# A key of their own for attention's values, values and next scores in one TensorE step, and a third buffer for x2's sums

## The chip, the cores and the metric

The kernel runs on one core of a Trainium2 chip, in one launch. The metric is the time of one execution on the device in microseconds (us). The same execution that was profiled gave the trace; all rows below come from it. TensorE is called PE in the rows, VectorE DVE, ScalarE ACT, GpSimd POOL and SyncE SP (it only issues DMAs here).

## The reference

Three layers follow each other on 8 sequences of 576 positions and 512 features, 4,608 positions in all.

```python
# attention, in chunks of 64 positions, 8 heads of 64
scores = scale * matmul(q_c, k_c.T)
scores = scores - max(scores)
attn = exp(scores);  attn = attn / (sum(attn) + 1e-9)
x = matmul(attn, v_c)
# first feed-forward
xn = (x - mu) / sqrt(var + 1e-6) * g_ln
x2 = x + maximum(xn @ w_ch1, 0) @ w_ch2
# gated layer
h = gelu(x2 @ w_in);  u, v = halves of h
v_n = (v - mu) / sqrt(var + 1e-6) * g_ln
v_s = w_sg @ v_n (over the 576 positions) + b_sg
out = x2 + (u * v_s) @ w_out
```

## The kernel before

**Tiles and stages.** The 4,608 positions are 36 tiles t of 128 rows; two tiles make one of 18 blocks b. Phase 1 does attention and the first feed-forward and writes x2 to a scratch tensor in HBM (`x2d`). Phase 2 does the gated layer in four groups of nine tiles and reads x2 back. Large products are computed in fp16 as a high and a low half, three matmuls for one; from block 4 on, and in phase 2, seven products of sub-blocks stand for eight, for which sums of sub-blocks are made first.

**Attention of a tile** (`attention`, lines 265 to 351). SP loads q and k into `qk` or `qkl` (L328) and v into `v` or `vl` (L329). TensorE makes the scores (L296, 16 matmuls of 64x64 in fp32; the rows count each as two), DVE takes their maximum (`mx`, L331) and subtracts it (`pm`, L332), ACT does the exponential (L335), TensorE transposes (L306), DVE sums (`sm`, L337, and L324, L325), ACT copies the transposed tile out (`pt`, L339), TensorE makes the values (L315, again 16 matmuls of 64x64), and DVE multiplies them into `x` (L345). `norm` follows: statistics (L376, L377), normalised `xn` (L379), its halves, and a transposing DMA into `xT`. From tile 6 on all tiles use one pair of PSUM banks, `pair1`: the scores lie in one half of each bank, the values in the other, but both halves have one key. So the scores of tile t+1 wait until `x` of tile t has been read.

**First feed-forward.** Blocks 0 to 3 run `ff1` (L537) and `ff2` (L558), with x2 put together at L570. From block 4 on `ff1p` (L647) writes bank 2 or 3, ACT takes it out (L662), DVE makes the sums (L669 to L671), ACT and POOL or DVE make the halves (L674, L676), and `ff2p` (L698) multiplies by the second weight. Each output tile is stored to `x2d` by SP (L576), and its largest value is taken (L203). Between block 3 and 4 `sums_w2` prepares the second weight (L592 and L602 on DVE, L607 and L608 on ACT, L611 and L612 on POOL). `prep` prepares the weights of phase 2; `par` (L229 to L241) turns a column of maxima into one number in all partitions, with two small TensorE steps, `turn` (L208) and `spread` (L220), and two DVE steps, `rowmax` (L212) and `floor` (L225). Late uses of `par` share `pair1`.

**Phase 2.** `x2_piece` loads two x2 tiles into a buffer `xs` (L919), DVE makes three sums (L926 to L928), ACT and DVE make the halves (L943, L953), and transposing DMAs follow (L941). A unit of v makes seven products (L1250), taken out by ACT (L1156) and DVE (L1160); then come v's ninth tile (L1275), u (L1292, L1313), the mixing over positions (L1346, L1347) and the output product (L1425), which DVE adds to `xr`, x2 loaded a second time (L1428, L1433).

**What sets the order.** Both phases are written as operations with an engine, an assumed duration, the keys they read and write, a priority and a distance `lat`, the assumed time until another engine may use the result. `Plan.run` plays this through: on each engine, of the operations that are ready at that time the one with the smallest priority goes next. The order thus made is fixed in the program; a step that comes late on the chip holds all that stand behind it on its engine. `plan` orders phase 1 and `plan2` phase 2.

Of the kernel before, what the change touches and what calls it, by code (L numbers as in the profile page):

```python
# [132 lines left out]
def fused_kernel(ctx: ExitStack, tc, qkv, w1, w2, g1, w_in, w_out, wsgt, wsgs, g2, b_sg, out):  # L133
# [95 lines left out]
    def par(dst, src, rd, wr, pr):  # L229

        nscr[0] += 1
        if pr < 1000:
            k, c = f"scr{nscr[0] % 3}", nscr[0] % 3 * 160
            scr = bank[6][:, c:c + 160]
        else:
            k, scr = "pair1", pair[1][:, 0, 0:160]
        pr = min(pr, 500)
        op("PE", 130, lambda: turn(scr, src), rd=rd + ["ident"], wr=[k], prio=pr, lat=300)
        op("DVE", 260, lambda: rowmax(scr), rd=[k], wr=["rowm"], prio=pr)
        op("PE", 130, lambda: spread(scr), rd=["rowm"], wr=[k], prio=pr, lat=300)  # L240
        op("DVE", 130, lambda: floor(dst, scr), rd=[k], wr=wr, prio=pr)  # L241
# [21 lines left out]
    xT_t = {}  # L263

    def attention(t):
        early = t < 8
        n = t % 2 if t < 6 else 1
        s2, ks = pair[n], f"pair{n}"
        pr = TUNE['a'][t] if t < 8 else 10 * t
        lat = TUNE['g'][2] if t < 8 else 300 if t < 12 else 1300  # L270
        z = 1

        def o(eng, ns, fn, **k):
            ns = COST.get((eng, ns), ns)
# [28 lines left out]

# [31 lines left out]
        o("ACT", 520, lambda: nc.scalar.activation(out=pm.t, in_=pm.t, func=AF.Exp, scale=0.125), wr=[pm])  # L335
# [7 lines left out]
        ), rd=[ks], wr=[pt])  # L343
        o("PE", 1260 * z, pv_, rd=[pt, v], wr=[ks])
# [5 lines left out]
        ), rd=[ks, rd], wr=[x])  # L350
# [432 lines left out]
    def prep(nm, srcs):  # L783
# [19 lines left out]
        op("DVE", 70, lambda: absmax(redc[:, i:i + 1], mxc[:, i, 0:n]), rd=[f"mxc{i}"], wr=[f"redc{i}"], prio=pr)  # L803

        def sums(k, uv):
            a, c = (full(k + 2 * y)[:, uv * 512:uv * 512 + 512].rearrange("p (h e) -> p h e", h=2) for y in range(2))
            t = winT(k, uv).rearrange("p a n e -> p (a n e)").bitcast(F32).rearrange("p (n e) -> p n e", n=4)
            for o, x, y in (
                (t[:, 0], a[:, 1], a[:, 0]), (t[:, 1], c[:, 1], t[:, 0]),
                (t[:, 2], c[:, 1], a[:, 1]), (t[:, 3], c[:, 0], t[:, 1]),  # L810
            ):
                nc.vector.tensor_tensor(out=o, in0=x, in1=y, op=ALU.subtract)

        if nm == "win":
            for k in range(2):
                for uv in range(2):
                    op("DVE", 1400, lambda k=k, uv=uv: sums(k, uv), rd=[ck[k], ck[k + 2]], wr=[f"winT{k}{uv}"], prio=pr)
# [83 lines left out]
    def x2_make(pl, g, p, pr):  # L901
# [67 lines left out]
    with tc.manual_schedule():  # L969
# [128 lines left out]
        gl = fixed("gl", 1, [P, 4, GT * P], F16)  # L1098
        fixed("hx", 4, [P, 7 * 256], F16)
# [451 lines left out]
```

## Time and profile before

| | |
|---|---|
| median of 3 runs | 1243.23 us (1242.81 to 1244.31) |
| the profiled execution | 1242.74 us |
| its span in the trace | 1241.0 us |
| TensorE busy | 1202.6 us, 97% |
| VectorE, ScalarE, GpSimd busy | 67%, 45%, 35% |
| TensorE clock, mean granted share | 0.992 |

TensorE's matmuls are pipelined, so a "busy" TensorE may still be slower than it could be; its idle time is what the gaps in its row show. The granted clock is 1.00 at 2.4 GHz and 0.50 at 1.2 GHz. A row of the waits names the instruction that waited and the one whose end released it.

### The profile page before, as it was taken

How to read it: one execution, taken by the hardware profiler on the slowest of the kernel's cores; microseconds unless marked ns; L12 is line 12 of the kernel's file. 1: busy time of each engine (PE TensorE's matmuls, PEld its weight loads, DVE VectorE, ACT ScalarE, POOL GpSimd, SP SyncE). 2: the span in 40 equal slices, each digit the busy share in tenths (PEclk: the TensorE clock that was granted, in tenths of full speed). 3: DMA queues.
4: the chain of work that ended last, by engine and by line, in shares of the span. 5: the costliest groups of instructions: out<-in, count | busy, mean ns of one | idle time of the engine just before them, and what ended most of it. 6: DMA issues, size and time to landing. Idle time of an engine off the chain costs nothing. (4 is left out here: it accounts for less than half of the span.)

```text
span 1241.0 us, 27021 instructions
## 1 busy us (share of the span) xinstructions
PE 1202.6 (97%) x11412; PEld 890.7 (72%) x11412; DVE 828.5 (67%) x1545; ACT 561.7 (45%) x844; POOL 439.4 (35%) x425
## 2 busy tenths in 40 slices
PE   7899999899999999999999999998999999999998
PEld 5688654678888888888888888887565357457453
DVE  7786124988967678646555665676688669558445
ACT  6676402455664474343433334344645435435321
POOL 3461401654555474434543344333302302302200
PEclk9999999999999999999999999999999899999999
DMA  9863002244321312322232120345146392382202
GB/s 325 243 200 111 1 34 67 71 167 137 119 69 53 78 43 87 83 56 64 58 69 61 52 61 18 81 109 152 38 104 160 108 170 79 110 137 69 85 1 85
DMA packets 140665, 118.33 MB, mean 95 GB/s; under 512 B 104960, under 2 KB 113152, under 8 KB 140544
## 3 DMA queue, kind: packets, MB, share of 16 engines
q1 hardware_dynamic: 140544, 116.61, 34.9%
q8 instruction: 89, 1.46, 0.5%
q14 instruction: 32, 0.26, 0.1%
HBM read 72.55 MB, written 18.87 MB: 74 GB/s over the span
## 5 line engine op out<-in xcount | busy, mean ns | idle before, releaser
L647 PE MATMUL bank<-xT,w1h 128*128 128x256 f16 x1792 | 302.3, 273 | 0.4 <-DVE x L570 0.4
L698 PEld LDWEIGHTS <-arena 128*128 128x128 f16 x2352 | 226.8, 98 | 30.0 <-DVE arena L676 0.9
L647 PE MATMUL bank<-xT,w1l 128*128 128x256 f16 x896 | 244.8, 273 | 0.0
L676 POOL TENSOR_TENSOR arena<-arena 128x896 f16<-128x896 f32 x69 | 130.9, 1897 | 222.7 <-ACT arena L674 212.9
L698 PE MATMUL acc<-w,arena 128*128 128x256 f16 x1344 | 202.8, 273 | 0.8 <-DVE arena L676 0.7
L647 PEld LDWEIGHTS <-w1h 128*128 128x128 f16 x1792 | 174.2, 98 | 22.5 <-issue 0.8
L674 ACT ACTIVATE arena<-arena 128x896 f16<-128x896 f32 x112 | 106.3, 949 | 166.6 <-DVE arena L671 78.1
L698 PE MATMUL acc<-w2s,arena 128*128 128x256 f16 x1008 | 165.3, 273 | 0.0
L669 DVE TENSOR_TENSOR arena<-arena 128x256 f32<-128x256 f32 x112 | 79.5, 710 | 110.5 <-ACT arena L662 110.3
L662 ACT ACTIVATE arena<-bank 128x512 f32<-128x512 f32 x112 | 66.4, 593 | 112.7 <-PE bank L647 112.0
L647 PEld LDWEIGHTS <-w1l 128*128 128x128 f16 x896 | 87.9, 98 | 10.4
L537 PE MATMUL bank<-xT,w1h 128*128 128x256 f16 x512 | 87.0, 275 | 4.9 <-DMA xT<-hl 4.0
L1197 POOL TENSOR_SCALAR rs<-mv 128x2 f32<-128x2 f32 (+1 forms) x20 | 4.7, 235 | 215.6 <-DVE mv L1192 215.3
L1250 PEld LDWEIGHTS <-x2T 128*128 128x128 f16 x672 | 66.0, 99 | 16.0 <-issue 6.0
L727 POOL TENSOR_TENSOR x<-x,u 128x256 f32<-128x256 f32 (+1 forms) x60 | 63.1, 1078 | 37.8 <-DVE x L717 23.9
L537 PE MATMUL bank<-xT,w1l 128*128 128x256 f16 x256 | 70.2, 274 | 0.0
L676 DVE TENSOR_TENSOR arena<-arena 128x896 f16<-128x896 f32 x43 | 57.0, 1325 | 12.8 <-ACT arena L674 12.8
L537 PEld LDWEIGHTS <-w1h 128*128 128x128 f16 x512 | 49.2, 98 | 16.1 <-DMA xT<-hl 4.2
L670 DVE TENSOR_TENSOR arena<-arena 128x256 f32<-128x256 f32 x112 | 55.8, 499 | 3.8
L1346 PEld LDWEIGHTS <-vh 128*128 128x128 f16 x288 | 28.2, 98 | 33.6 <-issue 0.9
L1346 PE MATMUL pb<-wsg,vh 128*128 128x512 f16 x166 | 51.9, 380 | 0.0
L1425 PEld LDWEIGHTS <-gh 128*128 128x128 f16 x288 | 27.7, 98 | 31.2 <-issue 0.9
(286 smaller groups left out, 2354.0 us busy)
## 6 DMA issues: line engine op xcount, KB each, us to landing
straw<-in_w SPq DMA_DIRECT2D x16, 1023.8 KB, 5.9
qkl<-in_qkv SPq DMA_DIRECT2D x26, 512.0 KB, 3.6
x2d<-x SPq DMA_DIRECT2D x36, 256.0 KB, 2.0
xs<-x2d SPq DMA_DIRECT2D x36, 256.0 KB, 3.4
xr<-x2d SPq DMA_DIRECT2D x36, 256.0 KB, 3.0
out<-xr SPq DMA_DIRECT2D x36, 256.0 KB, 3.1
vl<-in_qkv SPq DMA_DIRECT2D x26, 256.0 KB, 2.7
qk<-in_qkv SPq DMA_DIRECT2D x10, 512.0 KB, 5.9
```

The costliest lines, as they stand in the source:

```text
L537: nc.tensor.matmul(acc, lhsT=w[j][:, k, fc], rhs=xT.t[:, x, k], start=(n == 0), stop=(n == 11))
L647: nc.tensor.matmul(acc[:, y * 256:y * 256 + 256], lhsT=w[j][:, k, fc], rhs=xT.t[:, x, k], start=(n == 0), stop=(n == 11),)
L662: op("ACT", 600, lambda: nc.scalar.activation(out=o.t[:, 0:4].rearrange("p n t -> p (n t)"), in_=acc, func=AF.Relu, scale=0.5), rd=[kb] + ...
L669: nc.vector.tensor_tensor(out=two(6, 8), in0=two(1, 3), in1=two(0, 2), op=ALU.subtract)
L670: nc.vector.tensor_tensor(out=two(4, 7), in0=two(0, 6), in1=two(2, 8), op=ALU.add)
L674: op("ACT", 950, lambda: nc.scalar.activation(out=h.t[:, 0], in_=o.t[:, 1:8], func=AF.Copy), rd=[o] + ar, wr=[h], prio=-100)
L676: op(lo[0], lo[1], lambda: lo[2].tensor_tensor(out=h.t[:, 1], in0=o.t[:, 1:8], in1=h.t[:, 0], op=ALU.subtract), rd=[o], wr=[h], prio=-100)
L698: nc.tensor.matmul(acc, lhsT=h.t[:, x, n], rhs=r(y), start=(first and j == 0 and m == 0), stop=(j == 7 and m == 2), skip_group_check=True,)
L727: op("POOL", ns, lambda: nc.gpsimd.tensor_tensor(out=d(), in0=d(), in1=v(), op=ALU.add), rd=u + ["q6", "q5", "q7"], wr=[x], prio=-50)
L1250: nc.tensor.matmul(ap[:, q * 256:q * 256 + 256], lhsT=xT[:, x, a, k, c], rhs=right(b, 1, k, w), start=(first and n == 0), stop=(k == 1 and ...
L1346: nc.tensor.matmul(ap, lhsT=v[:, fc], rhs=w[:, 0:512], start=(n == 0), stop=end)
L1425: nc.tensor.matmul(ap, lhsT=x[:, k, c], rhs=w[:, k], start=(n == 0), stop=(n == 11))
```

## The change

Five edits go together.

1. In phase 2 the x2 sums get a third buffer `xz` beside the two `xs`. It lies where `xr` lay; `xr` goes to the other pool, with 5 buffers instead of 8. The assumed time of an `xs` load rises from 3300 to 6000.
2. From tile 10 on (`JOIN`) the values half of `pair1` has its own key, `pairv`. The scores of a tile are no longer an operation of their own there: the values of tile t and the scores of tile t+1 are one TensorE operation, 25 times.
3. The assumed distances of attention rise: 300 and 1300 become 600 (tiles 10 and 11) and 1000, the exponential and the copy of `pt` get 1500 and then 3000, the load of `qkl` 4000 instead of 2200.
4. Late uses of `par` write a part of the values half, under `pairv`, and their `rowmax` is assumed 3000 away; two maxima ahead of it get 4000 and 3000.
5. The sums of `win` in `prep` are two operations of 800 instead of one of 1400.

```diff
@@ par
+        slow = TUNE['g'][0]
...
-            k, scr = "pair1", pair[1][:, 0, 0:160]
+            k, scr, slow = "pairv", pair[1][:, 0, 256:416], 3000
...
-        op("DVE", 260, lambda: rowmax(scr), rd=[k], wr=["rowm"], prio=pr)
+        op("DVE", 260, lambda: rowmax(scr), rd=[k], wr=["rowm"], prio=pr, lat=slow)
@@ attention
+    started = {}
+    JOIN = 2 * B0 + 2
+
+    def scores(t, o):
+
+        a = palloc("qk", 2, [P, 2, 512], F32) if t < JOIN else palloc("qkl", 1, [P, 2, 512], F32)
+        src = qkv[t].rearrange("p (a f) -> p a f", a=3)
+        o("SP", 1460, lambda: nc.sync.dma_start(out=a.t, in_=src[:, 0:2]), wr=[a], lat=2200 if t < JOIN else 4000)
+        s2 = pair[t % 2 if t < 6 else 1]
...
+        kp = ks if t < JOIN else "pairv"
...
+        lat = TUNE['g'][2] if t < 8 else 300 if t < JOIN else 600 if t < JOIN + 2 else 1000
+        far = dict(lat=1500 if t < JOIN + 2 else 3000) if t >= JOIN else {}
...
-        o("PE", 1260 * z, pv_, rd=[pt, v], wr=[ks])
+        ), rd=[ks], wr=[pt], **far)
+        if t < JOIN or t + 1 == NT:
+            o("PE", 1260 * z, pv_, rd=[pt, v], wr=[kp])
+        else:
+            scores(t + 1, o)
+            a_, qk_ = started[t + 1]
+            o("PE", 1260, lambda: (pv_(), qk_()), rd=[pt, v, a_], wr=[kp, ks])
...
-        ), rd=[ks, rd], wr=[x])
+        ), rd=[kp, rd], wr=[x])
@@ x2_piece
-            ), rd=["xsL"] + [f"x2d{t}"] * (pl is plan), wr=[xs], lat=2200 if pl is plan else 3300, prio=pr)
+            ), rd=["xsL"] + [f"x2d{t}"] * (pl is plan), wr=[xs], lat=2200 if pl is plan else 6000, prio=pr)
@@ phase 2's buffers
-            ("vs", 2, [P, 512]), ("vt", 2, [P, 4, 64]), ("xr", 8, [P, D]),
+            ("vs", 2, [P, 512]), ("vt", 2, [P, 4, 64]),
...
+        fixed("xr", 5, [P, D])
+        x2p["xs"] += [fixed("xz", 1, [P, 9, 256])]
```

No instruction is added to or taken from TensorE. What the planner makes of the edits is shown at three places.

TensorE before, around the scores of tile 28 in the steady part of phase 1: `pair1` is attention's PSUM pair, `bank3` the output of `ff1p`, `w1h7` and `w1l7` the halves of the first weight's last part. The values of the same tile 27 stand 68 rows ahead, between matmuls of `ff1p` and `ff2p`.

```order
L647 MATMUL bank3_69<-xT_6328,w1h7_153 128x256
L647 LDWEIGHTS w1l7_161
L647 MATMUL bank3_69<-xT_6328,w1l7_161 128x256
L296 MATMUL pair1_67<-qkl_7258 64x64 x16
L647 LDWEIGHTS w1h7_153
L647 MATMUL bank3_69<-xT_6328,w1h7_153 128x256
```

The same engine after, at the scores of the same tile (there L716 is `ff2p`, L665 `ff1p`, L332 the values and L280 the scores; `acc` and `arena` are the output and input of `ff2p`):

```order
L716 MATMUL acc3_2803<-w2s1_2549,arena_117 128x256
L716 LDWEIGHTS arena_117
L716 MATMUL acc3_2803<-w2s1_2549,arena_117 128x256
L332 MATMUL pair1_67<-vl_6945,pt_7043 64x64 x16
L280 MATMUL pair1_67<-qkl_6962 64x64 x16
L665 LDWEIGHTS w1h4_150
L665 MATMUL bank2_68<-xT_6381,w1h4_150 128x256
```

The values of one tile and the scores of the next stand side by side, where 39 matmuls of 128x256 with their weight loads stood between them before.

DVE before, ahead of the first long wait of phase 2: `o11` and `hv1` are outputs of a unit of v, `pb0` to `pb2` its PSUM banks, L926 to L928 the sums of an x2 piece whose buffer a DMA fills.

```order
L1160 SCALAR_TENSOR_TENSOR o11_10712<-pb0_10760,e2g_130,o11_10712 128x512
L926 TENSOR_TENSOR xs0_10749<-xs0_10749 128x2x256
L927 TENSOR_TENSOR xs0_10749<-xs0_10749 128x2x256
L928 TENSOR_TENSOR xs0_10749<-xs0_10749 128x256
L1160 SCALAR_TENSOR_TENSOR hv1_10714<-pb1_10761,e2g_130,o11_10712 128x2x256
L1160 SCALAR_TENSOR_TENSOR hv1_10714<-pb2_10762,e2g_130,hv1_10714 128x2x256
```

DVE after, at the same unit (L945 to L947 are the sums, L972 the low halves of an earlier piece, `xz` the third buffer):

```order
L1181 SCALAR_TENSOR_TENSOR o11_10712<-pb0_10758,e2g_130,o11_10712 128x512
L972 SCALAR_TENSOR_TENSOR hx1_10755<-xz0_10753,i2g_131,hx0_10754 128x768
L1181 SCALAR_TENSOR_TENSOR hv1_10714<-pb1_10759,e2g_130,o11_10712 128x2x256
L945 TENSOR_TENSOR xs0_6083<-xs0_6083 128x2x256
L946 TENSOR_TENSOR xs0_6083<-xs0_6083 128x2x256
L947 TENSOR_TENSOR xs0_6083<-xs0_6083 128x256
L1181 SCALAR_TENSOR_TENSOR hv1_10714<-pb2_10760,e2g_130,hv1_10714 128x2x256
```

The sums stand behind the step that frees `pb1`, no longer ahead of it, and still ahead of the one that frees `pb2`.

DVE before, at the second long wait of phase 2: `uT` is u, transposed, `acc0` and `pb3` its PSUM banks.

```order
L1160 SCALAR_TENSOR_TENSOR uT0_10753<-pb3_10763,e2g_130,o10_10711 128x512
L926 TENSOR_TENSOR xs0_10749<-xs0_10749 128x2x256
L927 TENSOR_TENSOR xs0_10749<-xs0_10749 128x2x256
L928 TENSOR_TENSOR xs0_10749<-xs0_10749 128x256
L1160 SCALAR_TENSOR_TENSOR uT0_10753<-acc0_2808,e2g_130,uT0_10753 128x512
```

DVE after, at the same steps:

```order
L1181 SCALAR_TENSOR_TENSOR o10_10711<-pb2_10760,e2g_130,o10_10711 128x512
L1181 SCALAR_TENSOR_TENSOR uT0_10745<-pb3_10761,e2g_130,o10_10711 128x512
L1181 SCALAR_TENSOR_TENSOR uT0_10745<-acc0_2800,e2g_130,uT0_10745 128x512
L1181 SCALAR_TENSOR_TENSOR uT0_10745<-pb3_10761,e2g_130,o10_10711 128x512
L1181 SCALAR_TENSOR_TENSOR uT0_10745<-acc0_2800,e2g_130,o10_10711 128x512
```

No sums stand between the steps of u any more; those of `xz` are four steps ahead of the first row, before an output tile and the statistics of v.

## Rows read from the trace of the kernel before

**Rows 1.** Windows: stretch, us, busy PE, PEld, DVE, ACT, POOL (count), PEclk, DMA, GB/s.
```profile
205.00:262.00 57.00, 50.67 (x475) 33.92 (x474) 53.30 (x85) 27.16 (x40) 29.13 (x22) 0.97 0.30 93
...
330.00:485.00 155.00, 148.44 (x1700) 128.76 (x1698) 117.02 (x203) 85.02 (x120) 92.82 (x70) 1.00 0.24 64
485.00:757.00 272.00, 271.98 (x3151) 239.62 (x3149) 166.78 (x334) 104.81 (x152) 114.96 (x101) 1.00 0.24 60
...
840.00:990.00 150.00, 141.12 (x953) 84.19 (x951) 108.22 (x191) 73.86 (x97) 37.85 (x56) 0.97 0.45 116
```

**Rows 2.** TensorE's waits, 205 to 500 us: waiting line, releaser, total, times, longest.
```profile
PE pair L296 <- DVE x L345: 5.4, 3, 2.4
PE pair L315 <- ACT pt L339: 2.5, 4, 0.8
PE pair L306 <- ACT pm L335: 1.6, 2, 1.1
PE pair L220 <- DVE rowm L212: 1.5, 1, 1.5
```

**Rows 3.** Stretches at the low clock, and one after a wait that kept it.
```profile
252.23:255.64 3.41, 3.41 (x17) 2.45 (x18) 3.38 (x6) 0.52 (x1) 1.83 (x2) 0.50 0.55 180
951.96:955.37 3.41, 3.41 (x16) 2.12 (x15) 2.96 (x5) 3.36 (x5) 1.11 (x1) 0.50 0.12 41
979.27:986.10 6.83, 5.89 (x14) 2.02 (x14) 3.92 (x7) 3.43 (x3) 0.00 (x0) 0.50 0.00 0
...
854.50:858.00 3.50, 3.33 (x32) 2.83 (x30) 2.58 (x5) 1.60 (x2) 0.00 (x0) 1.00 0.88 212
```

**Rows 4.** DVE's timeline, 222 to 256 us: start, duration, operation.
```profile
231.22 0.41 DVE L602 TENSOR_TENSOR tf<-tf,bf 128x256 f32<-128x256 f32 x1
...
239.31 1.99 DVE L602 TENSOR_TENSOR tf<-bf,tf 128x256 f32<-128x256 f32 x1
...
250.78 0.68 DVE L345 TENSOR_TENSOR x<-pair,rd 128x512 f32<-128x512 f32 x1
```

**Rows 5.** TensorE's timeline around one values step of the steady part.
```profile
623.72 0.27 PE L647 MATMUL bank<-xT,w1l 128*128 128x256 f16 x1
623.93 0.69 PE L315 MATMUL pair<-vl,pt 64*64 64x64 f32 x32
624.55 0.50 PE L698 MATMUL acc<-w,arena 128*128 128x256 f16 x3
624.89 0.49 PE L698 MATMUL acc<-w2s,arena 128*128 128x256 f16 x3
```

**Rows 6.** TensorE's timeline, 12 to 14 us: scores and values side by side.
```profile
12.52 0.69 PE L296 MATMUL pair<-qk 64*64 64x64 f32 x32 [0.95 <-DVE x L345]
13.03 0.65 PE L315 MATMUL pair<-v,pt 64*64 64x64 f32 x32
```

**Rows 7.** TensorE's waits, 840 to 1000 us.
```profile
PE acc L1292 <- DVE uT L1160: 3.1, 1, 3.1
PE pb L1250 <- ACT o L1156: 2.8, 1, 2.8
PE pb L1250 <- DVE hv L1160: 2.4, 2, 2.2
```

**Rows 8.** DVE's timeline at the first of these waits.
```profile
948.20 0.69 DVE L926 TENSOR_TENSOR xs<-xs 128x512 f32<-128x512 f32 x1 [3.82 <-DMA xs<-x2d]
```

**Rows 9.** The chain that ended last: its two `xs` loads.
```profile
941.47 6.71 DMA xs<-x2d
...
973.14 4.51 DMA xs<-x2d
```

**Rows 10.** SP's, DVE's and TensorE's timelines around tile 28's `x`.
```profile
606.02 1.06 SPq L576 DMA_DIRECT2D x2d<-x  x2
...
608.85 0.68 DVE L345 TENSOR_TENSOR x<-pair,rd 128x512 f32<-128x512 f32 x1
...
611.62 0.69 PE L296 MATMUL pair<-qkl 64*64 64x64 f32 x32
```

More of the change, by code (lines that the diff above doesn't have):

```diff
@@ L302, in qk, with attention, o @@
                         )
+        started[t] = a, qk
+    def attention(t):
+        n = t % 2 if t < 6 else 1
+        s2, ks = pair[n], f"pair{n}"
+        kp = ks if t < JOIN else "pairv"
+        pr = TUNE['a'][t] if t < 8 else 10 * t
+        lat = TUNE['g'][2] if t < 8 else 300 if t < JOIN else 600 if t < JOIN + 2 else 1000
+        far = dict(lat=1500 if t < JOIN + 2 else 3000) if t >= JOIN else {}
+        z = 1
+        def o(eng, ns, fn, **k):
+            ns = COST.get((eng, ns), ns)
+            op(eng, ns, fn, prio=pr, lat=k.pop("lat", lat), **k)
+        if t not in started:
+            scores(t, o)
+            a, qk = started[t]
+            o("PE", 1260 * z, qk, rd=[a], wr=[ks])
+        v = palloc("v", 2, [P, 512], F32) if t < JOIN else palloc("vl", 1, [P, 512], F32)
+        o("SP", 730, lambda: nc.sync.dma_start(out=v.t, in_=qkv[t].rearrange("p (a f) -> p a f", a=3)[:, 2]), wr=[v], lat=2200)
+        mx = palloc("mx", 2, [P, 2, 4, 1], F32)
+        pm = palloc("pm", 2, [P, 4, 2, 64], F32)
+        sm = palloc("sm", 2, [P, 4, 2, 1], F32)
+        rd = palloc("rd", 2, [P, 4, 2, 1], F32)
+        pt = palloc("pt", 1, [P, 4, 128], F32)
+        if t < 2:
+            x = plan.buf(f"x{t}", 1, lambda: stage.tile([P, 512], F32, name=f"x{t}"))
+        else:
+            x = palloc("x", 6, [P, 512], F32, px)
+        sv = s2[:, :, 0:256].rearrange("p a (h k) -> p a h k", h=4)
+        pv = s2[:, :, 256:512].rearrange("p a (h d) -> p a h d", h=4)
         def pt_():
@@ L334, in attention @@
         ), rd=[ks, mx], wr=[pm])
-        o("ACT", 520, lambda: nc.scalar.activation(out=pm.t, in_=pm.t, func=AF.Exp, scale=0.125), wr=[pm])
+        o("ACT", 520, lambda: nc.scalar.activation(out=pm.t, in_=pm.t, func=AF.Exp, scale=0.125), wr=[pm], **far)
         o("PE", 850, pt_, rd=[pm, "ident"], wr=[ks])
@@ L802, in prep, with sums @@
             ), rd=[ck[k]], wr=[f"mxc{i}", junk], prio=pr)
[L803 to L805 removed]
+        op("DVE", 70, lambda: absmax(redc[:, i:i + 1], mxc[:, i, 0:n]), rd=[f"mxc{i}"], wr=[f"redc{i}"], prio=pr, lat=4000)
+        def sums(k, uv, y2):
             a, c = (full(k + 2 * y)[:, uv * 512:uv * 512 + 512].rearrange("p (h e) -> p h e", h=2) for y in range(2))
@@ L816, in prep @@
                 for uv in range(2):
-                    op("DVE", 1400, lambda k=k, uv=uv: sums(k, uv), rd=[ck[k], ck[k + 2]], wr=[f"winT{k}{uv}"], prio=pr)
+                    for y in range(2):
+                        op("DVE", 800, lambda k=k, uv=uv, y=y: sums(k, uv, y), rd=[ck[k], ck[k + 2]], wr=[f"winT{k}{uv}"], prio=pr)
         return lambda: halve(nm, n, i, m, q, full, ck)
@@ L961, in first_x2 @@
         pr = 9500
-        op("DVE", 100, lambda: absmax(redg[:, 0:1], x2mx[:, 0:GT]), rd=[f"x2mx{i}" for i in range(GT)], wr=["redg"], prio=pr)
+        op("DVE", 100, lambda: absmax(redg[:, 0:1], x2mx[:, 0:GT]), rd=[f"x2mx{i}" for i in range(GT)], wr=["redg"], prio=pr, lat=3000)
         par(e2g[:, 0:1], redg[:, 0:1], ["redg"], ["x2e"], pr)
```

31 lines of the change are left out of this document (2 added, 29 removed).

## Prediction

> **What bounds the kernel now.** I read the windows first, then TensorE's waits, then the timeline around each long wait. The windows [rows 1] part the span into stretches with different limits. From 485 to 757 us TensorE is busy 271.98 of 272 us: nothing waits there, and only less TensorE work can help. From 205 to 262 us it is idle for 57 - 50.67 = 6.33 us, and DVE, busy 53.30 of 57, is nearly a bound of its own. From 330 to 485 us it is idle for 6.56 us while DVE has 38 us to spare. From 840 to 990 us it is idle for 8.88 us. Ahead of 205 us and behind 990 us the order around the long waits stays, and I count nothing there. The waits [rows 2] say for what: the scores (L296) wait three times, 5.4 us in all, until the tile before has been read into `x`; the values wait for `pt`, the transposes for `pm`, and `spread` for `rowmax`. In phase 2 there are four waits [rows 7]: u for an evacuation on DVE (3.1 us), v for one on ACT (2.8) and for one on DVE (2.4 in two).
>
> Long waits cost twice. After the 2.4 us wait for `x` TensorE ran at 0.50, its lower level of 1.2 GHz, from 252.23 to 255.64 us; after the 2.2 us wait of v from 951.96 to 955.37, and after the 3.1 us wait of u from 979.27 to 986.10 [rows 3]. Work at half speed takes twice its time, so half of the busy time there is lost: 1.7, 1.7 and 5.89 / 2 = 2.9 us. The 2.8 us wait at 851 us was not followed by such a stretch: 854.50 to 858.00 has 1.00 [rows 3].
>
> **Part 1: scores no longer behind x (205 to 262 us).** Two of the three waits for `x` lie here, 1.95 us and 2.40 us as TensorE's timeline has them; `x` of the second was read at 250.78 [rows 4]. With a key for each half the scores follow the values at once and need `x` no more, so 4.35 us of waiting and 1.7 us of clock go, 6.05 us. But what is late next is DVE, on which every other step of the tile stands in line: it has only 57 - 53.30 = 3.70 us idle in this stretch, and the first joined pair stands 1.3 us later than the scores of tile 10 did (six matmuls of 128x512). Following the new order with the old durations, I find the first `ff1p` of block 5 some 5.4 us earlier, three joined pairs included. I take 5.4; the ends are 3.7 - 1.6 = 2.1 (see below) and 6.05 + 3 x 0.21 = 6.7.
>
> The lower end comes from the one DVE step that ran long: a sum of the second weight took 1.99 us at 239.31 and 0.41 at 231.22 [rows 4], 1.6 more, and GpSimd worked at the former time. One more such meeting in the new order takes 1.6 us from DVE's idle time. The Trainium skill (page "SBUF — State Buffer", section "SBUF: two separate sides") says that a GpSimd instruction and a VectorE instruction with two SBUF inputs exclude each other for a whole instruction; the long row agrees, and by that rule any order pays for the meetings it makes, so that this part would be 2.1 and the time 3.3 us more.
>
> **Part 2: attention's distances and the late maxima (330 to 485 us).** Of the 6.56 us of idle time here [rows 1], one wait is for `x` (the rest of 5.4, about 1.05), `spread` for `rowmax` is 1.5, values for `pt` two times 0.8, transposes for `pm` 1.1, and scores behind `floor` the rest [rows 2]. The first goes with the key. The other steps are planned with longer distances, so TensorE has other matmuls ahead of them, and `par` no longer stands between a tile's values and the next tile's scores; DVE's 38 us of slack says that it can be on time. Added wait: `par`'s steps now wait for `x`'s read under `pairv`, and behind `turn` on TensorE stand `ff1p` and `ff2p`; `x` is read within 0.68 us [rows 10], and one or two values steps behind a late `floor` may wait some tenths. I take 6.0 of 6.56; ends 4.5 and 6.5.
>
> **Part 3: joined steps.** One values step costs [rows 5]: from the start of the last normal matmul, 623.72, to its own start 0.21, of which 0.11 is the normal pitch (0.33 us for three matmuls, 624.55 to 624.89), and from there 0.62 to the next normal one. So 0.10 of lead-in and 0.62. Where scores and values stood side by side the second began 0.51 after the first [rows 6], not 0.62, and has no lead-in of its own. A joined pair saves 0.11 + 0.10 = 0.21 us. There are 25 pairs, three of them in part 1: 22 x 0.21 = 4.6 us. As the stretch from 485 to 757 us has no idle time, this is on the path. Ends: 22 x 0.15 = 3.3 if the lead-in stays in part, 22 x 0.26 = 5.7.
>
> **Part 4: x2's sums (944 to 986 us).** The wait of v comes from DVE's order: the sums of a piece stood ahead of the step that frees a bank and began at 948.20, when the load that was issued at 941.47 had landed, 6.71 us later [rows 8, 9]; DVE was idle 3.82 us for it. The third buffer lets loads go out a piece earlier, and in the new order the step that frees `pb1` is ahead of the sums, so that TensorE goes on; it needs `pb2` one product of 1.3 us later. At the u wait the load took 4.51 us from 973.14 [rows 9]; there the sums have left the place altogether. Gain: 2.2 + 3.1 of waiting and 1.7 + 2.9 of clock = 9.9 us; the first place may keep up to 1.3. I take 9.3; ends 7.5 (1.3 of wait and some clock stay) and 9.9. The loads that move earlier meet the transposing DMAs on SP's queue; five `xr` buffers instead of eight hold the last loads back, but in the last 30 us those of `xr` still land over 4 us before their use by my count, so I put that at nothing; its cover gone, it would cost what the load is late.
>
> **Left as they are.** The wait of 2.8 us at 851 us [rows 7] is behind the store of the last x2 tile, which the change does not move. It has one new risk: that it now is followed by a stretch at half clock, 1.7 us. The split sums of `win` and the longer distances of the maxima move DVE work that has slack: nothing.
>
> **The sum.** 5.4 + 6.0 + 4.6 + 9.3 = 25.3 us from the profiled execution's 1242.74, which is 0.5 us under the median of 1243.23. Every stretch gets a new order, and the rows cannot show the waits that it makes; I set 3 us aside for them, the size of one long wait of [rows 2] with half of its clock. So 1243.2 - 25.3 + 3 = 1220.9; I say 1221. All lower ends give 2.1 + 4.5 + 3.3 + 7.5 = 17.4, and 1226; all upper ends 28.8, and 1214.5.
>
> **Rivals.** *The x2 loads stay late* (chance 0.13): the loads wait behind transposes in SP's queue, or the sums reach a new place at which a bank waits. For it: the same load of 256 KB took 6.71 and 4.51 us [rows 9]. Against: a whole buffer more. Then part 4 gives little: 1221 + 7 = about 1228.
>
> *The new order waits elsewhere* (0.08): in parts 1 and 2 only places of waiting change. For it: DVE is full up to 262 us [rows 1]. Only parts 3 and 4 and about half of the clock remain: 1243 - 14 = about 1229 to 1232.
>
> *Slower* (0.02). Joined steps stand earlier, and the values of tile t+1 wait for `x` of tile t. `x` of tile 28 started at 608.85, just as the second store issued from 606.02 on had landed and freed its buffer, and ended at 609.53; the scores of tile 29 started at 611.62 [rows 10], and the joined step that now needs this read stands 12 matmuls of 0.11 earlier, 1.3 us, at about 610.3. The margin is 0.7 us, in each of seven blocks. If stores landed 3.5 us later, every block would wait 2.8 us and lose 1.7 us of clock: 7 x 4.5 = 31 us against 25, about 1249. From 22 / 7 = 3.1 us a block on, that is stores about 2.1 us late, the gain is gone. Against: nothing in the change delays stores.
>
> *The gaps stay under other names* (0.03): then nothing but part 3 remains and is eaten by new waits, about 1242.
>
> *Short waits lower the clock* (0.04): the waits that remain, two or three under 1 us, are each followed by a stretch at half clock, 1.7 us each: 1224 to 1227. Against: from 330 to 485 us waits of up to 1.5 us, 6.56 in all, kept a clock of 1.00 [rows 1, 2]. The Trainium skill (page "TensorE: Matmul & The Clock Gate", section "A second HAM failure mode: psum-queue depth-cycling") says that TensorE pausing briefly between groups of matmuls is enough to make the clock swing; that stretch speaks against it here.
>
> **How the numbers follow.** The forecast has 0.70; with the rivals this makes 1. The forecast's own bounds are 1214.5 to 1226, and to leave out no more than 2 in 10 I go on to the rival of late loads: 1214 to 1230. A measurement of this kernel tells apart about 0.2%, 2.5 us. Faster: all but the last cases, 0.95; within 0.2%: 0.03; slower: 0.02.
>
> **What would show it.** In the profile after: no wait of L280 (the scores) for `x`; at 205 to 262 us no stretch at 0.50; a step of values and scores in a row with about 1.2 us between its normal neighbours; idle time of TensorE from 330 to 485 us under 2 us; in phase 2 no wait of u for `uT`, and at most 1.3 us of v for `hv`. It is wrong if new waits of 2 us or more stand in the steady stretch, if `xs` loads still hold DVE ahead of an evacuation, or if joined pairs cost twice 0.72.

## The result, and the profile after

The changed kernel takes 1229.72 us (median, 1228.32 to 1230.56) where the kernel before took 1243.77 in the same comparison: a ratio of 0.9885, 95% interval 0.9868 to 0.9902. That is faster by 1.15%. It is inside the range of the prediction, by 0.3 us at the upper end, and 8.7 us above its likeliest value: of a gain of 22.2 us, 14 came.

These are the windows of the kernel after, over the same stretches as [rows 1] (stretch, length, busy time of PE, PEld, DVE, ACT and POOL with counts, PE clock, DMA share, GB/s):

```profile
205.00:262.00 57.00, 52.40 (x515) 36.80 (x514) 53.09 (x83) 26.58 (x39) 30.08 (x22) 1.00 0.30 93
...
330.00:485.00 155.00, 146.88 (x1731) 127.92 (x1734) 129.34 (x216) 85.64 (x123) 97.29 (x74) 0.99 0.25 69
485.00:757.00 272.00, 272.00 (x3116) 242.00 (x3108) 161.28 (x333) 106.95 (x154) 121.75 (x102) 1.00 0.21 58
...
840.00:990.00 150.00, 148.16 (x1060) 89.10 (x1061) 117.26 (x197) 77.88 (x104) 35.82 (x55) 1.00 0.49 121
```

The last stretch has lost nearly all of its idle time: 8.88 us before, 1.84 now. The first still has 4.6 us of idle time and 53 us of VectorE. The second has more idle time than before, 8.1 us for 6.56, and VectorE worked there 129.3 us where it worked 117.0. About half of that is more steps in the stretch, 216 for 203; the rest is longer steps: the second sum of `ff1p` (L688), for one, took 726 ns a piece from 262 to 505 us where it had taken 551. Between the first two stretches idle time is new; this is the window before, then after:

```profile
262.00:330.00 68.00, 67.96 (x800) 59.35 (x799) 58.23 (x108) 40.48 (x60) 32.33 (x28) 1.00 0.53 162
```

```profile
262.00:330.00 68.00, 65.88 (x812) 58.08 (x811) 60.72 (x107) 39.75 (x60) 32.51 (x26) 1.00 0.57 164
```

TensorE's waits in the same stretches, beside [rows 2] and [rows 7], first from 205 to 500 us, then from 820 to 1050 us (waiting line and its releaser, total, times, longest; L323 is the transposes, L332 the values, L208 `turn`, L363 `x`):

```profile
PE pair L323 <- DVE x L363: 3.2, 1, 3.2
PE pair L332 <- ACT pt L352: 3.0, 3, 1.7
PE pair L208 <- DVE mx L344: 2.1, 1, 2.1
PE acc L716 <- DVE u L735: 1.7, 4, 0.9
PE bank L665 <- DVE x L588: 1.5, 1, 1.5
...
PE pair L208 <- DVE pm L345: 0.7, 1, 0.7
```

```profile
PE acc L716 <- POOL arena L694: 1.2, 1, 1.2
PE acc L1313 <- DVE uT L1181: 1.1, 1, 1.1
PE pb L1271 <- DVE hv L1181: 1.1, 2, 0.7
PE acc L716 <- DVE arena L694: 0.7, 1, 0.7
```

In these stretches no scores wait for `x` any more. In their place a transpose does, for 3.2 us, and `turn` waits for `x` and `mx`.

To see where the time went I matched the two traces at equal TensorE work (the moments at which the same amount of fp16 matmul columns had been issued) and took the differences by stretch. The borders are times of the kernel before; the joined pairs are counted where they stand (6 ahead of 330 us, 19 behind it). Attention's own matmuls are fp32 and not in the count: at 330 us the kernel after is one scores step (0.6 us) further than the one before, which belongs to the stretch ahead of 330 us and stands in the one behind it.

| stretch of before | predicted gain | after |
|---|---|---|
| to 209 us | 0 | 1.0 |
| 209 to 330 (part 1 and 3 pairs more) | 6.0 | 2.2 |
| 330 to 828 (part 2 and 19 pairs) | 10.0 | 2.0 |
| 828 to 908 (the wait at 851) | 0 | 0.7 |
| 908 to 1021 (part 4) | 9.3 | 9.3 |
| the rest | 0 | -0.8 |
| set aside for new waits | -3.0 | |
| sum | 22.3 | 14.4 |

Ahead of 209 us the profiled executions of all kernels here lie between -1.6 and +2.0 us of the one of before; below I compare stretches, which repeat within some tenths (209 to 330 us within 0.7, the second execution of the changed kernel shows). The kernel before was timed anew beside each group of runs: 1241.58 us for e1 to e4, 1244.66 for e5 to e8, 1242.82 for e9 to e12. So runs of different groups are compared by their ratios; 0.0010 of a ratio is 1.24 us.

### The profile page after: what moved, and what is told of

The parts are those of the page before. It is cut to its first block, busy times and chain, and to the rows that moved or that the text cites. A ratio compares the mean times of both kernels' runs of the same rounds, so it can differ in the third digit from the quotient of the medians.

```text
span 1226.5 us, 26988 instructions
## 1 busy us (share of the span) xinstructions
PE 1191.2 (97%) x11412; PEld 887.6 (72%) x11412; DVE 841.0 (69%) x1545; ACT 559.0 (46%) x844; POOL 449.3 (37%) x425
## 3 DMA queue, kind: packets, MB, share of 16 engines
q8 instruction: 89, 1.46, 0.5%
## 5 line engine op out<-in xcount | busy, mean ns | idle before, releaser
L665 PE MATMUL bank<-xT,w1h 128*128 128x256 f16 x1792 | 301.3, 273 | 1.7 <-DVE x L588 1.5
L716 PEld LDWEIGHTS <-arena 128*128 128x128 f16 x2352 | 227.9, 98 | 35.4 <-issue 2.8
L665 PE MATMUL bank<-xT,w1l 128*128 128x256 f16 x896 | 244.9, 273 | 0.0
L716 PE MATMUL acc<-w,arena 128*128 128x256 f16 x1344 | 202.9, 273 | 5.2 <-POOL arena L694 1.9
L665 PEld LDWEIGHTS <-w1h 128*128 128x128 f16 x1792 | 174.8, 98 | 23.5 <-issue 2.5
L687 DVE TENSOR_TENSOR arena<-arena 128x256 f32<-128x256 f32 x112 | 75.7, 676 | 131.2 <-ACT arena L680 131.0
L716 PE MATMUL acc<-w2s,arena 128*128 128x256 f16 x1008 | 165.4, 273 | 0.0
L665 PEld LDWEIGHTS <-w1l 128*128 128x128 f16 x896 | 87.8, 98 | 10.4
L694 DVE TENSOR_TENSOR arena<-arena 128x896 f16<-128x896 f32 x43 | 60.4, 1405 | 13.7 <-ACT arena L692 13.7
L688 DVE TENSOR_TENSOR arena<-arena 128x256 f32<-128x256 f32 x112 | 64.7, 578 | 3.8
L402 POOL TENSOR_TENSOR hl<-xn,hl 128x512 f16<-128x512 f32 x33 | 43.6, 1320 | 29.3 <-ACT hl L400 29.3
```

What stands on the lines that cost most here:

```text
L665: nc.tensor.matmul(acc[:, y * 256:y * 256 + 256], lhsT=w[j][:, k, fc], rhs=xT.t[:, x, k], start=(n == 0), stop=(n == 11),)
L687: nc.vector.tensor_tensor(out=two(6, 8), in0=two(1, 3), in1=two(0, 2), op=ALU.subtract)
L688: nc.vector.tensor_tensor(out=two(4, 7), in0=two(0, 6), in1=two(2, 8), op=ALU.add)
L694: op(lo[0], lo[1], lambda: lo[2].tensor_tensor(out=h.t[:, 1], in0=o.t[:, 1:8], in1=h.t[:, 0], op=ALU.subtract), rd=[o], wr=[h], prio=-100)
L716: nc.tensor.matmul(acc, lhsT=h.t[:, x, n], rhs=r(y), start=(first and j == 0 and m == 0), stop=(j == 7 and m == 2), skip_group_check=True,)
```

## The experiments

Four groups of runs follow: what the two stretches of phase 1 lack (e1, e2, e5, e6), one half of the change without the other (e3, e4), single edits undone (e7, e8), and versions that might beat both (e9 to e12). "Gain" is by the matching at equal work against the kernel before.

| run | median us | ratio to before, 95% interval | 209-330 | 330-828 | 828-908 | 908-1021 |
|---|---|---|---|---|---|---|
| after | 1229.72 | 0.9885 (0.9868 to 0.9902) | 2.2 | 2.0 | 0.7 | 9.3 |
| e1 both keys | 1220.81 | 0.9833 (0.9804 to 0.9862) | 2.9 | 9.8 | 0.6 | 9.3 |
| e2 no reads | 1222.60 | 0.9842 (0.9817 to 0.9866) | 3.0 | 7.3 | 0.7 | 9.3 |
| e3 phase 2 only | 1232.96 | 0.9926 (0.9903 to 0.9949) | -0.7 | 0.0 | 2.0 | 9.3 |
| e4 phase 1 only | 1240.00 | 0.9986 (0.9974 to 0.9997) | 2.9 | 2.0 | -4.2 | 1.1 |
| e5 no reads, w2 | 1219.10 | 0.9803 (0.9773 to 0.9833) | 10.2 | 3.7 | 0.6 | 9.3 |
| e6 keys, no reads | 1222.56 | 0.9825 (0.9793 to 0.9858) | 2.9 | 9.5 | 0.9 | 9.3 |
| e7 old par | 1223.95 | 0.9837 (0.9806 to 0.9868) | -1.0 | 10.9 | 1.4 | 9.3 |
| e8 old distances | 1223.45 | 0.9837 (0.9803 to 0.9871) | 0.8 | 8.5 | 1.4 | 9.3 |
| e9 after again | 1229.23 | 0.9889 (0.9866 to 0.9911) | 2.9 | 1.9 | 1.0 | 9.3 |
| e10 keys, old distances | 1228.94 | 0.9884 (0.9861 to 0.9906) | -0.1 | 5.1 | 1.5 | 9.3 |
| e11 keys, VectorE lows | 1218.63 | 0.9804 (0.9784 to 0.9825) | 7.7 | 7.8 | 1.2 | 9.3 |
| e12 keys, long sums | 1220.57 | 0.9822 (0.9797 to 0.9846) | 3.7 | 8.9 | 1.5 | 9.3 |

**What the runs were for.** The 3.2 us wait in the kernel after reads like this. First DVE's timeline (start, duration, operation), then ACT's, then TensorE's, then the window that follows it:

```profile
470.70 0.68 DVE L345 TENSOR_TENSOR pm<-pair,mx 128x512 f32<-128x512 f32 x1
...
474.41 1.84 DVE L694 TENSOR_TENSOR arena<-arena 128x896 f16<-128x896 f32 x1 [0.50 <-ACT arena L692]
476.17 0.68 DVE L363 TENSOR_TENSOR x<-pair,rd 128x512 f32<-128x512 f32 x1
```

```profile
471.41 0.63 ACT L348 ACTIVATE pm<-pm 128x512 f32<-128x512 f32 x1 [1.48 <-DVE pm L345]
```

```profile
476.99 0.63 PE L323 MATMUL pair<-ident,pm 128*128 128x128 f32 x4 [3.18 <-DVE x L363]
```

```profile
477.90:481.20 3.30, 3.30 (x18) 2.34 (x16) 2.97 (x7) 1.31 (x2) 1.08 (x1) 0.50 0.50 160
```

The transpose has its input since the exponential ended at 472.04. It stands until `x` of the tile before has been read, although it writes the scores' half and `x` reads the values' half; and a stretch at half clock follows. In the built program this instruction waits for VectorE and for ScalarE:

```
L323 MATMUL pair1_67<-ident_124,pm_6017 128x128 [waits DVE_49,Activation_49]
```

So the program still orders the two halves of `pair1`. The change took that order out of the planner by giving the halves two keys, and in seven tiles the planner now has VectorE read `x` behind the next tile's `pm`, which from tile 8 on it never did before. The 3.2 us wait is at the first of the seven; at the other six no transpose waits. The Trainium skill (page "PSUM — Partial Sum Buffer", section "PSUM bank collisions raise a hardware error") says that two engines may not access one PSUM bank in the same 32 partitions at the same time, whatever the columns. By that the order of the two steps is not one to be taken away; no run here took it away. The wait of `turn` is of the same kind in its last 0.6 us: its input `redc` was there at 328.92 us; it needed `x`'s read, which ended at 335.14 and which the planner knows of, since both are in the values' half; and then it stood for `mx`, in the scores' half, which the planner does not know of. DVE's rows, then TensorE's:

```profile
328.77 0.15 DVE L203 TENSOR_REDUCE redc<-mxc 128x1 f32<-128x2 f32 x1 [1.22 <-ACT tmp L818]
...
334.46 0.68 DVE L363 TENSOR_TENSOR x<-pair,rd 128x512 f32<-128x512 f32 x1
335.06 0.68 DVE L344 TENSOR_REDUCE mx<-pair 128x8 f32<-128x512 f32 x1
```

```profile
335.79 0.38 PE L208 MATMUL pair<-ident,redc 128*1 128x128 f32 x2 [2.15 <-DVE mx L344]
```

That made theory H: the order the planner no longer knows costs the time. Theory D is that VectorE is late because GpSimd lengthens its steps.

**e1, both keys named.**

```diff
-        o("PE", 850, pt_, rd=[pm, "ident"], wr=[ks])
+        o("PE", 850, pt_, rd=[pm, "ident"], wr=[ks] if kp == ks else [ks, kp])
...
+        ko = [k, "pair1"] if k == "pairv" else [k]
-        op("PE", 130, lambda: turn(scr, src), rd=rd + ["ident"], wr=[k], prio=pr, lat=300)
+        op("PE", 130, lambda: turn(scr, src), rd=rd + ["ident"], wr=ko, prio=pr, lat=300)
```

`spread` writes `ko` too.

> The changed kernel, with the planner told that the transposes from tile 10 on, and the two TensorE steps of the late maxima, write under both keys of pair1, the scores' and the values'. Theory H (halves): in the changed kernel the built program still orders the two halves against each other, which the planner no longer knows, so that a transpose waited 3.2 us for x of the tile before and a turn waited 0.75 and 0.6 us for pm and mx; told of it, the planner puts them later and 4.5 us go: about 1225. Rival D (VectorE): these waits only show that VectorE is late there, since its steps run beside GpSimd's; the order of the keys changes where TensorE waits and not how long: 1228 to 1231.

Measured: 1220.81, a ratio of 0.9833 where the kernel after has 0.9885, which is 6.5 us less; 9.8 us were gained from 330 to 828 us, where 10.0 had been predicted. No step waits across the halves any more; `turn` waits for its own maximum. Its waits from 205 to 500 us begin so, and its window from 330 to 485 us:

```profile
PE pair L333 <- ACT pt L353: 3.0, 3, 1.7
PE pair L208 <- DVE redc L203: 1.6, 1, 1.6
```

```profile
330.00:485.00 155.00, 152.42 (x1755) 133.93 (x1753) 116.31 (x211) 86.09 (x126) 96.21 (x74) 1.00 0.22 65
```

The gain is larger than H's 4.5 us, and VectorE's time fell to 116.3 us with the order: H alone was not isolated.

**e2, the same order without GpSimd's reads.** The output lacks the low halves of phase 2's weights.

```diff
-            op("POOL", 2100 * m // 1024, lambda half=half, view=view, tmp=tmp: nc.gpsimd.tensor_tensor(
-                out=half(1), in0=view(tmp.t[:, 0:m]), in1=half(0), op=ALU.subtract
-            ), rd=[tmp], wr=[key], prio=pr)
+            op("POOL", 2100 * m // 1024, lambda half=half, view=view, tmp=tmp: nc.gpsimd.memset(half(1), 0.0), rd=[tmp], wr=[key], prio=pr)
```

> The changed kernel in the same order, but the low halves of phase 2's weights, which GpSimd makes by a subtraction of two 128x1024 operands in 2.2 to 2.3 us, are set to zero by GpSimd without reading anything; the low halves are left out of the result. Theory D: VectorE's sums, 2.23 us beside such a subtraction and 0.42 us alone, get short, VectorE's busy time from 330 to 485 us falls from 129 by 10 or more, and the waits for u (1.5 us in three), for x and for the transpose fall by half or more: about 1224. Theory H: the transposes' wait stays, since it is for x, and the time is within 1.5 us of 1229.7.

Measured: 1222.60, by the ratios 5.3 us under the kernel after, and 7.3 us from 330 to 828 us, as D expects. In the kernel after, one GpSimd subtraction and a VectorE sum beside it (POOL's row, then DVE's), and then the same sum and the next one in e2:

```profile
456.72 2.31 POOL L884 TENSOR_TENSOR winT<-tmp,winT 128x1024 f16<-128x1024 f32 x1
```

```profile
457.08 2.23 DVE L688 TENSOR_TENSOR arena<-arena 128x256 f32<-128x256 f32 x1
```

```profile
455.03 0.42 DVE L688 TENSOR_TENSOR arena<-arena 128x256 f32<-128x256 f32 x1
460.38 0.43 DVE L688 TENSOR_TENSOR arena<-arena 128x256 f32<-128x256 f32 x1
```

VectorE's time from 330 to 485 us is 107.9 us there. Against H's expectation the 3.2 us wait of the transpose is gone as well, since `x` is no longer late; the `turn` still waits 2.15 us for `mx`. So in this order the transpose's wait takes both: an order that the planner does not know, and a VectorE that is late.

**e6, both.** The edits of e1 and e2 together (the same low halves left out).

> Both keys named to the planner, and phase 2's low halves set to zero without reading (left out of the result). With the meetings gone, what is left between this and the order of e2_no_reads is theory H alone. H: the wait of 2.15 us at the first turn falls to that for its own maximum, 1.5 at most, and nothing waits across the halves: 0.6 to 3 us under e2's 1222.6. Rival: meetings were all of it, and the time is e2's within 1.

Measured: 1222.56 with 9.5 us from 330 to 828 us, 2.2 us more than e2 and no more than e1. The ratios, 0.9825 for e2's 0.9842, are 2.1 us apart, with intervals that overlap and a start that scatters as much; the stretch shows H's gain over e2, and it is the cleanest measure of the keys: 2.2 us with these meetings gone, the lower part of what H expects. How e1's 7.8 us over the kernel after divide between the keys and the fewer meetings of its order stays open.

**e5, the same for the second weight.** The low halves of its sums are left out.

```diff
-            nc.gpsimd.tensor_tensor(out=w2s[j][:, 1], in0=tf.t[:, 1:4], in1=w2s[j][:, 0], op=ALU.subtract)
-            nc.gpsimd.tensor_tensor(
-                out=w[:, 0, 1, 256:512], in0=tf.t[:, 0], in1=w[:, 0, 0, 256:512], op=ALU.subtract
-            )
+            nc.gpsimd.memset(w2s[j][:, 1], 0.0)
+            nc.gpsimd.memset(w[:, 0, 1, 256:512], 0.0)
```

> The changed kernel in the same order, but the low halves of the second weight's sums (eight pairs of GpSimd subtractions between 205 and 290 us) are set to zero by GpSimd without reading; they are left out of the result. Theory D for part 1: the VectorE steps that meet them (1.99 and 2.1 us instead of 0.41) get short, the waits of TensorE from 225 to 290 us (6.4 us) fall by 2 or more: 1226.5 to 1228. Rival C (the chain of one tile: VectorE, ScalarE and TensorE in turn): the waits for pt of 0.9, 0.4 and 1.7 us and the one for x2 of 1.5 us stay, and the time is within 0.7 of 1229.7.

Measured: 1219.10, 10.2 us gained from 209 to 330 us instead of 2.2; none of the waits that the kernel after had from 225 to 290 us is left. More than D expected. DVE's rows of the kernel after, the same steps in e5, and a GpSimd row of the kernel after:

```profile
215.32 0.69 DVE L344 TENSOR_REDUCE mx<-pair 128x8 f32<-128x512 f32 x1 [0.92 <-issue]
...
218.14 1.26 DVE L620 TENSOR_TENSOR tf<-bf 128x256 f32<-128x256 f32 x1
...
226.93 1.62 DVE L341 TENSOR_SCALAR sm<-sm 128x8 f32<-128x8 f32 x1
...
232.93 1.27 DVE L203 TENSOR_REDUCE x2mx<-x 128x1 f32<-128x512 f32 x2
```

```profile
217.55 0.69 DVE L344 TENSOR_REDUCE mx<-pair 128x8 f32<-128x512 f32 x1 [0.91 <-issue]
...
219.89 0.42 DVE L620 TENSOR_TENSOR tf<-bf 128x256 f32<-128x256 f32 x1
...
225.81 0.16 DVE L341 TENSOR_SCALAR sm<-sm 128x8 f32<-128x8 f32 x1
...
230.01 1.27 DVE L203 TENSOR_REDUCE x2mx<-x 128x1 f32<-128x512 f32 x2
```

```profile
226.23 2.28 POOL L629 TENSOR_TENSOR w2s<-tf,w2s 128x768 f16<-128x768 f32 x1 [1.91 <-ACT w2s L625]
```

The same steps in the same order take 17.6 us in the one and 12.5 in the other. This run also shortened GpSimd's own work, so the 8 us are meetings and GpSimd's time together; e11 below leaves GpSimd less work in another way and gains 7.7 us there. The 3.2 us wait of the transpose for `x` is still in e5, and with it the small gain behind 330 us.

**e3 and e4, one half alone.** e3 is the kernel before with the phase 2 edits (edit 1 of the change), e4 the changed kernel with them undone.

> The kernel before with only the edits of phase 2: third sums buffer, five xr buffers in the other pool, xs loads at 6000. If parts add up, as the alignment of the two traces at equal work says (9.3 us between 930 and 995 us): 1243.8 - 9.3 = 1234.5, with the waits of u and v and both half-clock stretches gone. Rival: the phase 2 gain needs the earlier arrival of phase 1's last tiles, then 1237 to 1241.

> The changed kernel with the phase 2 edits undone: two sums buffers, eight xr, loads at 3300. If parts add up: 1229.7 + 9.3 = 1239, both long waits of phase 2 with their half-clock stretches back. Rival: 1233 to 1236 if phase 1's edits move the loads of phase 2 as well.

Measured: e3 1232.96 (0.9926, a gain of 9.2 us), near what adding up gives. e4 1240.00 (0.9986) gains 1.7 us where adding up gives 4.8: both expectations missed. Part 4's 9.3 us is the phase 2 edits alone: e3 has it to the tenth, with no half-clock stretch from 908 to 1021 us, and e4 has 1.1 us of it. What e4 lacks beside it is the stretch from 828 to 908 us, where it loses 4.2 us: the wait at 851 us is longer, a slow clock follows it (0.61 from 851.4 to 855 us, the risk that the prediction named for this place), and a wait of 1.4 us stands ahead of it. Without the phase 2 edits the rest of the change is hardly worth anything. e4's waits from 820 to 1000 us show the waits for `uT` and for `o` back and longer, and DVE idle 4.57 us for a load ahead of the sums:

```profile
PE acc L1311 <- DVE uT L1179: 5.5, 1, 5.5
PE pb L1269 <- ACT o L1175: 4.2, 1, 4.2
```

```profile
976.81 0.69 DVE L945 TENSOR_TENSOR xs<-xs 128x512 f32<-128x512 f32 x1 [4.57 <-DMA xs<-x2d]
```

**e7, the late maxima as before.** In this kernel `turn` writes over scores that have not been read yet, so a few tiles' attention is changed; its time stands for the order alone.

```diff
-            k, scr, slow = "pairv", pair[1][:, 0, 256:416], 3000
+            k, scr = "pair1", pair[1][:, 0, 0:160]
```

The distances of 4000 and 3000 of the two maxima are undone too.

> The changed kernel with the late maxima as before: in the scores' half under pair1, with the old distances. If the turns' waits (2.15, 0.68 and 0.75 us) are what that edit brought, 1226. Rival: the old waits come back (spread for rowmax 1.5, scores behind floor 0.2, 0.6 and 0.6 us), 1229 to 1231.

Measured: 1223.95 (0.9837, 6 us less than the kernel after); both expectations missed. It gains 10.9 us from 330 to 828 us, and 3.2 us less from 209 to 330; `spread` now waits 2.75 us, to 330.6. The maxima's own place in the values' half is what the joined step needs, not a gain in itself. No transpose waits for `x` here, although the planner has not been told of the order of the halves.

**e8, attention's old distances.**

```diff
-        lat = TUNE['g'][2] if t < 8 else 300 if t < JOIN else 600 if t < JOIN + 2 else 1000
-        far = dict(lat=1500 if t < JOIN + 2 else 3000) if t >= JOIN else {}
+        lat = TUNE['g'][2] if t < 8 else 300 if t < JOIN + 2 else 1300
+        far = {}
```

The `qkl` load goes back to 2200.

> The changed kernel with attention's old distances (300, 1300, the qkl load 2200, nothing longer for the exponential and the copy). If the longer distances are worth what the prediction gave them, the waits for pt and pm come back at more places: 1232 to 1236, and the steady stretch from 485 to 757 us is no longer without idle time. Rival: the joined order gives the slack by itself, 1229 to 1231.

Measured: 1223.45, by the ratios 6 us faster than the kernel after; both expectations missed. The waits for `pm` do come back, one of 3.6 us with a half-clock stretch, to 264.9, but no transpose waits for `x`, and the steady stretch stays without idle time. VectorE reads `x` behind the next tile's `pm` in ten tiles here, more than the seven of the kernel after: such an order does not make a wait by itself. Its waits from 205 to 500 us, first rows:

```profile
PE pair L323 <- ACT pm L348: 6.6, 4, 3.6
PE pair L332 <- DVE c_win_e L225: 1.8, 1, 1.8
PE pair L208 <- DVE pm L345: 0.8, 1, 0.8
```

**e9 to e12.** e9 is the changed kernel again. e10 has the edits of e1 and of e8. e11 has e1's and lets VectorE make the low halves for odd j; e12 has e1's and tells the planner 1700 and 2600 for the two VectorE steps of the second weight's sums.

```diff
@@ e11
+        e = nc.vector if j % 2 else nc.gpsimd
...
-        op("POOL", 2300, lo, rd=[tf], wr=[k], prio=pr)
+        op(*(("DVE", 1450) if j % 2 else ("POOL", 2300)), lo, rd=[tf], wr=[k], prio=pr)
```

> The changed kernel once more, beside the three that follow: 1228 to 1231, with the wait of a transpose for x of about 3.2 us near 477 us again, if that wait belongs to the order and not to one execution.

> Both keys named to the planner, and attention's old distances. If the keys are what part 2 lacked, no transpose waits for x here either and the time is near e1's, 1220 to 1223; if the longer distances are needed with it, the waits for pm and pt return and it is 1224 to 1228.

> Both keys named, and every second one of the low halves of the second weight's sums made by VectorE instead of GpSimd. Each costs VectorE about 1.4 us and takes away the meetings with its sums (1.6 us a meeting, by e5 some 8 us in all for eight): VectorE is full in that stretch, so between 1218 and 1222, no better than 2 us under e1's 1220.8.

> Both keys named, and the planner told longer durations for VectorE's two steps of the second weight's sums (1700 and 2600 instead of 1140 and 1300), about what they take beside GpSimd. If the waits from 225 to 290 us come from an order made with durations that the chip does not keep, they fall by 2 to 4 us: 1217 to 1219. Rival: VectorE is full there in any order, 1220 to 1222.

Measured: e9 1229.23 with the same wait of 3.18 us at the same place, and every other wait behind 205 us within 0.3 us: the waits belong to the order. e10 1228.94, a little above its second expectation: with the keys named the short distances cost 3.0 us in part 1 and 4.7 behind it, with the waits for `pm` back, so the longer distances are worth something there; without the keys named (e8) they had cost 5 us net from 209 to 828 us. e12 1220.57, as its rival said: the waits of part 1 go to the second weight's halves, which `ff2p` now waits for. e11 1218.63 has the lowest ratio of those that compute everything, 0.9804, with an interval that does not meet that of the changed kernel; it does meet those of e1, e8 and e12. By the ratios it is 3.6 us under e1, more than the 2 that had been expected. Its one long wait behind 205 us is that of the first `turn`, 3.2 us ending at 328; from 330 to 485 us TensorE is never idle in it:

```profile
330.00:485.00 155.00, 155.00 (x1771) 136.50 (x1770) 118.29 (x208) 88.85 (x129) 99.55 (x73) 0.99 0.24 73
```

## Why the prediction was right, and where it was not

The direction and the phase 2 part were right; 1221 was 8.7 us too low, from phase 1. That 1229.7 lies in the range is luck: its upper end of 1230 was taken from the rival of late x2 loads, which did not happen, and the forecast's own ends were 1214.5 (28.8 from 1243.2 is 1214.4) and 1226. Of the signs that it named, the scores no longer wait for `x`, no half-clock stretch stands from 205 to 262 us, and joined steps take 1.2 us; but TensorE is idle 8.1 us from 330 to 485 us, not under 2, and u still waits 1.1 us for `uT`. e1, which differs from the changed kernel in the planner's keys alone, gains 20.8 us.

- **Part 1** (5.4, ends 2.1 and 6.7): by 262 us some 5 us are gained, and by 330 us 2 to 3 of them are lost again. The prediction's own mark, the first `ff1p` of block 5, comes 2.4 us earlier (3.3 less the 0.9 gained ahead of 209 us; 2.5 in e9), not 5.4. The waits for `x` and the half-clock stretch went, as predicted, but waits for `pt`, `x2` and the halves of 6 us took their place; the longest stands behind 262 us, where the kernel before had 0.04 us of idle time and the prediction counted no wait:

```profile
264.76 0.70 PE L332 MATMUL pair<-vl,pt 64*64 64x64 f32 x32 [1.71 <-ACT pt L352]
```

The step that failed is "following the new order with the old durations": the order meets GpSimd elsewhere, and durations with it. The lower end had been drawn from one such meeting, and it proved nearer than the value taken. But the prediction read "the one DVE step that ran long" wrongly: there were more of them in the kernel before, such as

```profile
223.61 1.61 DVE L324 TENSOR_SCALAR sm<-sm 128x8 f32<-128x8 f32 x1
```

so that 2.1 and 2.4 are near each other is partly luck. e5, with 10.2 from 209 to 330 us, shows that these meetings and GpSimd's own time hold the stretch; it does not part the two. The rule of the Trainium skill (page "SBUF — State Buffer", section "SBUF: two separate sides"), by which the prediction put the part at 2.1, agrees with the 2.23 and 0.42 us of the sum with and without GpSimd's reads.
- **Part 2** (6.0 of 6.56): the failed term. Idle time rose to 8.1 us. The prediction named the added wait for `par` but held that with two keys the scores "need `x` no more", and priced nothing else that would; it did not ask what the program itself still orders. The transposes of the next tile do need `x`'s read. This, and a VectorE whose steps lasted longer beside GpSimd, made the new waits; with the keys named the stretch gave 9.8 of the 10.0 predicted with its pairs. It gave 10.9 in e7 and 8.5 in e8 as well, with the keys not named, so naming them is one cure of this order and not the only one; what the keys alone are worth is best shown with the meetings gone, 2.2 us.
- **Part 3** (0.21 a pair): mechanism and size were right. This is a joined pair on TensorE's timeline of the kernel after:

```profile
607.49 0.49 PE L716 MATMUL acc<-w2s,arena 128*128 128x256 f16 x3
607.91 0.69 PE L332 MATMUL pair<-vl,pt 64*64 64x64 f32 x32
608.42 0.65 PE L280 MATMUL pair<-qkl 64*64 64x64 f32 x32
609.00 0.39 PE L665 MATMUL bank<-xT,w1h 128*128 128x256 f16 x2
```

The three matmuls of the first row take 0.33 us, so the next normal one would have started at 607.82; it starts at 609.00, 1.18 us later. Two single steps of 0.72 would be 1.44: by these rows a pair saves 0.26, the upper end. Over a whole stretch it is less: from 500 to 757 us, where neither kernel's TensorE waits, the 11 pairs of the kernel after gain 2.1 us (with attention's steps counted in, at the prices of single steps), some 0.19 each. (Between the values of tile 27 and the scores of tile 28 there stood 33 matmuls in the program of before, not 39.)
- **Part 4** (9.3): 9.3 in every kernel with the phase 2 edits; 8.2 of them are theirs behind the new phase 1, where e4 has 1.1 without them.
- **Left as it was**: the wait at 851 us. The prediction put it to the store of the last x2 tile, which the change does not move. It is gone in the kernel after. What had waited for that store was ScalarE's evacuation `o` of v. In the built program of before, the buffers of `o` lie where phase 1 had its `x` buffers, so the first `o` may not be written until the last `x` has been stored; with edit 1, which takes `xr` out of the pool that holds `o`, they lie over halves of the first weight (`w1h5` to `w1h7`), and `o` waits for TensorE alone. The built programs of e3 and e4 agree: e3 has the new place and no such wait, e4 the old place and a wait of 4.2 us. ScalarE's row before, and after:

```profile
853.42 0.69 ACT L1156 ACTIVATE o<-pb,e2g 128x512 f32<-128x512 f32 x1 [7.73 <-DMA x2d<-x]
```

```profile
843.66 0.69 ACT L1177 ACTIVATE o<-pb,e2g 128x512 f32<-128x512 f32 x1 [0.60 <-PE pb L1271]
```

That gave 2.0 us in e3, net of a new wait of 1.1 us of u for `uT` behind it. In the kernel after it gave 0.7, since a new wait of 1.2 us for `arena` stands ahead of it as well.
- **The allowance** of 3 us for unseen waits was too small: the traces fall 10.9 us short of the 25.3 that the parts add up to (25.3 - 14.4). Of the rivals, "the new order waits elsewhere" (1229 to 1232, given 0.08) is what happened, in both parts of phase 1. The slower case did not show: from 485 to 757 us TensorE is busy 272.00 of 272, so no joined step waited for `x`. The x2 loads came in time.

## What to carry to other kernels

When a planner's key is split, look at what the built program still orders: a dependence that the planner does not know puts steps where they wait. Durations taken from the old order hold only as long as the same engines meet; where VectorE is nearly full, price a new order by the worst of its neighbours. Single edits to such a planner do not add up in phase 1 (by the ratios, old distances gained 6 us without the keys and lost 6 with them), while the edits that remove named waits of phase 2 were worth much the same at their place (part 4: 9.3 us alone, 8.2 behind the new phase 1). And a wait can belong to the place of a buffer in memory: moving a buffer took one away that no one had aimed at.

## What the runs showed of the hardware that was not expected

A wait of the same length at the same place can keep the clock or lose it. `turn`'s wait of 2.15 us kept a clock of 1.00 from 330 to 340 us in the kernel after, and again in its second execution (e9); the same wait in the same order in e2 had a mean of 0.83 there. What decides it stays open. Windows of the kernel after and of e2:

```profile
330.00:340.00 10.00, 6.82 (x59) 5.52 (x59) 9.81 (x17) 6.36 (x14) 5.13 (x5) 1.00 0.25 95
```

```profile
330.00:340.00 10.00, 7.77 (x54) 5.88 (x54) 9.37 (x15) 4.59 (x10) 5.14 (x5) 0.83 0.15 54
```

A VectorE step on 128x8 elements, L341, took 1.62 us beside a GpSimd subtraction and 0.16 without one (rows of e5 above). That is 1.46 us more, where the sum of 128x256 elements took 1.81 us more: the meeting costs a small step nearly as much as a large one here.
